# The last row of each reversed half: from the sync queue to the GpSimd queue, two steps behind the indirect store

## The chip, the cores and the metric

The kernel runs on one core of a Trainium2 chip. The metric is the device time of one execution in microseconds (us). The kernel before took 2382.77 us, the median of three runs (2381.13 to 2389.46).

## The reference

Eight batches of attention whose 12 heads are mixed before and after the softmax ("talking heads"), followed by a Fourier mixing of the result, a normalisation and a two-layer network:

```python
scores = scale * np.matmul(q, k.transpose(0, 1, 3, 2))      # q, k, v: 8 x 12 x 448 x 64
scores = np.einsum('bhij,hg->bgij', scores, w_pre)
attn = softmax(scores)
attn = np.einsum('bhij,hg->bgij', attn, w_post)
x = np.matmul(attn, v)                                      # to (8, 448, 768)
X = np.fft.fft(np.fft.fft(x, axis=1), axis=2)
u = x + np.real(X)
un = (u - mean(u)) / np.sqrt(var(u) + 1e-06)
out = u + np.maximum(un @ w_ch1, 0.0) @ w_ch2               # 768 -> 3072 -> 768
```

Everything is float32; the two weight matrices arrive as 64-bit floats and are converted on the chip.

## The kernel before, in words

There are two stages. The mixing stage computes `u` and leaves it in DRAM; the network stage (from 840 us on) reads it back and does the rest. Only the mixing stage and the passage into the network stage matter here.

**Steps.** Each batch is cut into 8 blocks of query rows and the blocks into 23 steps, so 8 batches make 184 steps. One step treats 4 x 5 rows of scores of all 12 heads. A loop over the step number `s` runs a list of actions (`ORDERS`, one list for even and one for odd `s`) and works on several steps at once:

- `emit_gather(s + 4)` (L496): four DMAs of 60 x 448 floats each (105 KB) copy the scores `Sb` of a step into the layout `Kr`, in which heads lie along partitions. All are issued by SyncE's queue (SP). `Kr` has three buffers.
- `emit_premix(s + 2)` (L507): TensorE multiplies `Kr` by the first mixing matrix, 16 small matmuls.
- `emit_max(s + 2)` (L514, VectorE), `emit_exp(s + 2)` (L521, ScalarE), `emit_scale(s + 2)` (L531, GpSimd): softmax.
- `emit_postmix(s)` (L541, TensorE) and `emit_turn(s)` (L554, VectorE): second mixing and a transposition.
- Fillers between them: the products of q and k (L479), whose results ScalarE copies to `Sb` (L342), products with v (L571), Fourier matmuls (L615, L680, L696), and the conversion of weights, one VectorE operation a step.

So a gather is issued in the loop two steps ahead of the matmuls that read it. TensorE, VectorE, ScalarE and GpSimd run exactly in the order in which the program is written; SP's queue is ordered by the framework's scheduler. GpSimd also issues the loads of q, k and v of the next batch (L425, L434), the loads and stores of weights (L225, L233) and does part of the Fourier folding (L636 to L657).

**The store.** When the last Fourier product of a batch's half has been added (`done` in `emit_s2`, L707 and L709), the closure `store` is put on the list `later`. In the `scale` action of each step, after `emit_scale`, the loop runs as many entries of `later` as stood there when the step began. `store` handles two tiles `X` of 113 rows. One goes to `u_scr` by an ordinary DMA (L728, SP). The other holds rows in reverse order and goes to `u_rev` by an indirect DMA (L719, GpSimd) that scatters 112 rows through the table `rows`. In the second half of a batch (`pair` 1) the tile has one row more, number 112, for row 112 of `u_rev`. Its DMA (L725) is what the change touches: 768 floats, once per batch, issued by SP. Because both DMAs write the tensor `u_rev[b]`, the framework lets L725 wait until the indirect store has landed.

In SP's order L725 stands behind one gather after L728 (batches 0, 2, 4) or behind two (batches 1, 3, 5), with the next gather right behind it. For batches 6 and 7 the store comes after the last step: batch 6 at the passage into the network stage, ahead of the first loads of `u` (L946, `load_u`), and batch 7 inside the first tile of the network stage. There the list `later` is emptied at once by `part`, or for batch 6 by the last turns of the loop and `part`.

Of the kernel before, what the change touches and what calls it, by code (L numbers as in the profile page):

```python
# [33 lines left out]
GR = SH // 2  # L34
# [268 lines left out]
def mix_phase(ctx, tc, rest, ident, q, k, v, w_pre, w_post, u_scr, u_rev, wts):  # L303
# [6 lines left out]
    nc = tc.nc  # L310
# [28 lines left out]
    pend, folds, later = [], [], []  # L339
# [14 lines left out]
    def ms_tile():  # L354
        return ms[-1]()
# [332 lines left out]
    def emit_s2(b, pair, par):  # L688

        st = batches[b]  # L690
        n, i0 = PR[pair], pair * GR
        ps = ms_tile()
        for y in range(2):
            w, _ = FOLD[par][par ^ y]
            for ch in range(2):
                nc.tensor.matmul(ps[:n, y:DH + 1:2],  # L696
                                 st["z", par, par ^ y][:w, ch, i0:i0 + n],
                                 tcs[:w, par, y, ch, :DQ + 1 - y],
                                 start=(ch == 0), stop=(ch == 1))

        def done():
            for back in range(2):
                X = groups[b * NG + 2 * pair + back]["X"]
                sub, add = (ALU.subtract, ALU.add) if par else (ALU.add, ALU.add)
                if back:
                    sub, add = add, sub
                nc.vector.tensor_tensor(X[:n, 0:DH + 1], X[:n, 0:DH + 1],  # L707
                                        ps[:n, 0:DH + 1], op=sub)
                nc.vector.tensor_tensor(X[:n, DH + 1:DM], X[:n, DH + 1:DM],  # L709
                                        ps[:n, DH - 1:0:-1], op=add)  # L710
            if par == 0:
                return
            later.append(store)

        def store():
            for back in range(2):
                X = groups[b * NG + 2 * pair + back].pop("X")
                if pair ^ back:
                    nc.gpsimd.indirect_dma_start(  # L719
                        out=u_rev[b][:, :],  # L720
                        out_offset=bass.IndirectOffsetOnAxis(
                            ap=rows[:GR, pair:pair + 1], axis=0),
                        in_=X[:GR, :], in_offset=None)
                    if pair:
                        later.append(lambda X=X: nc.sync.dma_start(  # L725
                            out=u_rev[b][GR:GR + 1, :], in_=X[GR:GR + 1, :]))
                else:
                    nc.sync.dma_start(  # L728
                        out=u_scr[b][pair * (SH + 1):pair * (SH + 1) + GR, :],
                        in_=X[pair:pair + GR, :])  # L730
        return [done]
# [674 lines left out]
```

## Time and profile before

| | |
|---|---|
| median of three runs | 2382.77 us |
| the profiled execution | 2392.76 us, its span 2391.0 us |
| PE / DVE / ACT / POOL busy, share of the span | 96% / 70% / 46% / 47% |
| mixing matmuls L507 | 2944, 554 ns mean, 221.2 us |
| gathers L496, all issued by SP | 736 of 105 KB; about 0.77 us of SP each |
| indirect stores L719 | 16, of 1042 ns on GpSimd; landing 4.1 to 5.9 us after their start |
| row stores L725 | 8, of 0.23 us on SP, at 255.6, 358.5, 457.3, 561.0, 663.2, 766.9, 833.6 and 915.6 us |
| loads by GpSimd in the mixing stage | L425 0.73 us, L434 0.63 us of GpSimd each |

The profiled execution took 10 us more than the median. Times inside it are counted from the span's start. PE is TensorE, DVE VectorE, ACT ScalarE, POOL GpSimd; a q behind an engine's name (SPq) means its sequencer, which issues DMAs and waits. In a timeline a bracket at the end of a row gives the idle time of the engine before it and what ended it.

### The profile page before, as it was taken

The numbers are of one execution on the slowest core, as the hardware profiler recorded it, in microseconds if no ns is written. First come the engines' busy times: TensorE is split into PE (matmuls) and PEld (weight loads), VectorE is DVE, ScalarE is ACT, GpSimd is POOL, SyncE is SP. The second block draws the span as 40 slices with busy tenths as digits, with TensorE's granted clock in tenths as the row PEclk, the third lists the DMA queues.
The fourth block names the chain that finished last, engine by engine and source line by source line (L and its number), as shares of the span: only waits on it lengthen the run. The fifth ranks groups of instructions, "written<-read, shape, count | busy, mean of one in ns | idle before, by whom it ended". The sixth has DMA issues, their size and how long they took to land.

```text
span 2391.0 us, 59448 instructions
## 1 busy us (share of the span) xinstructions
PE 2292.0 (96%) x22600; PEld 1717.7 (72%) x22600; DVE 1669.0 (70%) x3596; ACT 1100.5 (46%) x3085; POOL 1125.2 (47%) x1672
## 2 busy tenths in 40 slices
PE   6999999999999859999999999999999999999998
PEld 2455554554555547777777779999899999999998
DVE  3768786786877636776676767677767777776556
ACT  4767766676666522232122224444443444444444
POOL 3587877877776441211234343334333433344333
PEclk9999999999999979999999999999999999999999
DMA  7565554655645545656888794568466747674553
GB/s 159 158 177 175 175 176 144 198 165 163 187 156 163 203 131 169 223 189 234 242 245 218 215 307 114 165 176 242 133 161 178 219 135 189 160 219 118 146 126 67
DMA packets 213385, 425.60 MB, mean 178 GB/s; under 512 B 38766, under 2 KB 135430, under 8 KB 213102
## 3 DMA queue, kind: packets, MB, share of 16 engines
q1 hardware_dynamic: 142446, 280.38, 34.0%
q0 software_dynamic: 64656, 139.45, 26.8%
q8 instruction: 181, 2.97, 0.5%
q10 hardware_dynamic: 6000, 1.97, 0.5%
q14 instruction: 102, 0.84, 0.1%
HBM read 213.16 MB, written 129.39 MB: 143 GB/s over the span
## 4 chain that ended last, share of the span: by engine, by line
PE 52%; issue 6%; POOL 3%; DMA 2%; DVE 2%; ACT 0%; SPq 0%; POOLq 0%; DVEq 0%
PE psP L1062 15%; PE psP L1192 10%; PE psR L1062 8%; PE psR L1192 5%; PE psQ L1062 4%; PE psP L1135 4%; PE psQ L1192 3%; PE psR L1135 2%; PE psQ L1135 1%; POOL w L233 1%; DMA u<-u 1%; PE psQ L996 0%; DMA w1t<-w 0%; POOL raw L225 0%; DMA w<-wst 0%
## 5 line engine op out<-in xcount | busy, mean ns | idle before, releaser
L1062 PE MATMUL psP<-ub,w1t 128*128 128x256 f32 x2016 | 480.4, 379 | 1.2 <-DVE h L1081 1.2
L1062 PEld LDWEIGHTS psP<-ub,w1t 128*128 128x128 f32 x2016 | 379.0, 190 | 49.4 <-DVE h L1081 1.6
L531 POOL TENSOR_SCALAR PP<-PP,rcp 128x448 f32<-128x448 f32 x368 | 234.1, 645 | 230.2 <-DVE rcp L529 190.8
L514 DVE TENSOR_REDUCE nmx<-mx 128x1 f32<-128x448 f32 x368 | 213.7, 619 | 158.7 <-PE mx L507 153.7
L521 ACT ACTIVATE PP<-mx,nmx 128x448 f32<-128x448 f32 x368 | 230.3, 631 | 197.3 <-DVE nmx L514 187.4
L1226 POOL DMA_DIRECT2D out_dram<-od x109 | 132.9, 1394 | 282.5 <-DVE od L1223 159.5
L1026 POOL TENSOR_TENSOR hq<-h 128x256 f32<-128x256 f32 (+1 forms) x168 | 104.2, 620 | 292.4 <-ACT h L1082 172.0
L507 PE MATMUL mx<-Kr,kw 60*32 60x448 f32 x2944 | 221.2, 554 | 21.3 <-DMA Kr<-Sb 19.9
L1062 PE MATMUL psR<-ub,w1t 128*128 128x256 f32 x1008 | 232.9, 381 | 0.0
L1223 DVE TENSOR_TENSOR od<-od 128x768 f32<-128x768 f32 x196 | 188.6, 974 | 52.1 <-ACT od L1220 50.2
L1062 PEld LDWEIGHTS psR<-ub,w1t 128*128 128x128 f32 x1008 | 192.6, 191 | 26.4
L479 PE MATMUL ms<-kT,qT 64*32 64x448 f32 (+1 forms) x3072 | 202.3, 549 | 7.9 <-ACT qT L342 6.5
L554 DVE STREAM_TRANSPOSE Pv<-po 128x896 f32<-128x896 f32 x184 | 203.7, 1107 | 5.5 <-PE po L541 3.3
L342 ACT COPY Sb<-ms 124x448 f32<-124x448 f32 (+1 forms) x384 | 184.3, 540 | 48.8 <-PE ms L479 25.2
L541 PE MATMUL po<-PP,kw 60*32 60x448 f32 x2944 | 196.4, 541 | 0.0
L1220 ACT COPY od<-psP 128x192 f32<-128x192 f32 x390 | 124.7, 320 | 146.1 <-PE psP L1192 141.6
L571 PEld LDWEIGHTS ms<-Pv,vv 64*64 64x64 f32 x5376 | 137.0, 132 | 69.2 <-issue 52.3
L225 POOL DMA_DIRECT2D raw<-in_moe_w_ch_dram x88 | 53.4, 609 | 270.1 <-DVE tmp L269 252.4
L571 PE MATMUL ms<-Pv,vv 64*64 64x120 f32 (+1 forms) x5376 | 158.7, 263 | 0.4 <-ACT X L342 0.4
L1135 PE MATMUL psP<-w2t,h 128*128 128x384 f32 x448 | 153.8, 486 | 1.4 <-DVE od L1155 1.4
L1081 DVE TENSOR_TENSOR h<-h,psP 128x512 f32<-128x512 f32 x42 | 28.8, 687 | 142.0 <-PE psP L1062 141.6
L1135 PEld LDWEIGHTS psP<-w2t,h 128*128 128x128 f32 x448 | 84.1, 190 | 54.9 <-DVE od L1155 2.0
(143 smaller groups left out, 4497.3 us busy)
## 6 DMA issues: line engine op xcount, KB each, us to landing
ub<-ub SPq DMA_DIRECT2D x294, 384.0 KB
Kr<-Sb SPq DMA_DIRECT2D x736, 105.0 KB
out_dram<-od POOLq DMA_DIRECT2D x137, 384.0 KB, 8.7
w1t<-w SPq DMA_DIRECT2D x42, 384.0 KB
w2t<-w SPq DMA_DIRECT2D x42, 384.0 KB
raw<-in_moe_w_ch_dram POOLq DMA_DIRECT2D x56, 256.0 KB, 4.2
raw<-in_moe_w_ch_dram POOLq DMA_DIRECT2D x32, 384.0 KB, 5.0
w<-wst POOLq DMA_DIRECT2D x92, 128.0 KB, 4.3
```

Source lines behind the costliest of these rows:

```text
L479: nc.tensor.matmul(pss[x][o:o + hi - lo, :S], st["qT", xx][64 * x:64 * x + 64, y, lo:hi], st["kT", xx][64 * x:64 * x + 64, y, :], start=Tr ...
L507: nc.tensor.matmul(mx[x][64 * z + o:64 * z + o + 32, :S], kw1[64 * x:64 * x + KR, o:o + 32], Kr[64 * x:64 * x + KR, z, :], start=True, sto ...
L514: nc.vector.tensor_reduce(nmx[:, :], steps[T]["mx"][x][:, :S], axis=AX.X, op=ALU.max, negate=True)
L521: nc.scalar.activation(steps[T]["PP"][:, x, :], steps[T]["mx"][x][:, :S], ACTF.Exp, bias=steps[T]["nmx", x][:, :], accum_out=steps[T]["den ...
L531: nc.gpsimd.tensor_scalar(PP[:, x, :], PP[:, x, :], rcp[:, x:x + 1], 1.0, op0=ALU.mult, op1=ALU.mult)
L541: nc.tensor.matmul(po[o:o + 32, z, :S], kw2[64 * z:64 * z + KR, y, :], PP[64 * z:64 * z + KR, :, c * HS:(c + 1) * HS], start=True, stop=True)
L554: nc.vector.transpose(turned[a]["Pv"][:, j, :].rearrange("p (z s) -> p z s", z=2), steps[T]["po"][:, :, :S])
L571: nc.tensor.matmul(pss[y][64 * x:64 * x + 64, :nu * R], st["v", pr][64 * y:64 * y + 64, x, jb * D:(jb + 1) * D], _ap(Pv, 64 * y * rp + 32 ...
L1062: nc.tensor.matmul(p[:, m, :], w1[i][:, kc, m * P:(m + 1) * P], ub[:, kc, :], start=i in (0, 4, 1)[:3 - seed] and m == kc == 0, stop=kc == ...
L1135: nc.tensor.matmul(p, h[:, LHS[i], kf, x * P:(x + 1) * P], w2[i][:, kf, :], start=i in (0, 4, 1)[:3 - (c > 0)] and kf == 0, stop=kf == FM ...
L1192: nc.tensor.matmul(ps[j, key][:, :DQ], a, b, start=m in (0, 4), stop=True, skip_group_check=True)
L1223: eng.tensor_tensor(D[j][:, :, :], D[j][:, :, :], D[k][:, :, :], op=ALU.add)
```

## The change

The single row's DMA is issued by GpSimd instead of SP, and one level of delay is put around it: in place of the DMA itself, the list `later` gets a function that puts the DMA on `later` once more.

```diff
                     if pair:
-                        later.append(lambda X=X: nc.sync.dma_start(
-                            out=u_rev[b][GR:GR + 1, :], in_=X[GR:GR + 1, :]))
+                        later.append(lambda X=X: later.append(lambda: nc.gpsimd.dma_start(
+                            out=u_rev[b][GR:GR + 1, :], in_=X[GR:GR + 1, :])))
```

In step `t` `store` issues the indirect DMA, in `t + 1` the outer function runs, in `t + 2` the DMA is issued, after that step's two scale operations (L531). In the resulting order of instructions TensorE, VectorE and ScalarE have the same sequence as before. SP has eight DMAs fewer and gathers follow each other where L725 stood. GpSimd has eight DMAs more: in batches 0, 2 and 4 between the scale operations and the next loads of v and q, in batches 1, 3 and 5 between the scale operations and a folding operation (L636), in batch 6 behind both indirect stores, a small memset and two weight loads, with three more weight loads behind it, and in batch 7 directly behind the second indirect store. The row is written as 16 pieces of 48 floats there, where SP's form was one piece of 768. It still waits for the landing of the indirect store[...].

## Prediction

> **What bounds the kernel now.** I read the page first, then SP's waits, then the timelines of SP, TensorE and GpSimd around each row store, and last the chain of waits at the passage into the network stage. On the page TensorE is the bound nearly everywhere, and the mixing matmuls wait for gathers:
>
> ```profile
> span 2391.0 us, 59448 instructions
> ...
> L507 PE MATMUL mx<-Kr,kw 60*32 60x448 f32 x2944 | 221.2, 554 | 21.3 <-DMA Kr<-Sb 19.9
> ```
>
> With the weight loads of the same line the view by tile puts 61.6 us of TensorE's idle time down to gathers that had not landed. The next view is SP's own waits from 200 to 930 us (us in total, times, longest), the one after it the indirect store by its line:
>
> ```profile
> SPq L725 <- DMA v<-X,rows: 28.7, 8, 5.4
> ```
> ```profile
> DMA to landing us min/median/max: 4.1/4.8/5.9
> ```
>
> So SP stands still for 28.7 us in all until the indirect store has landed. Behind L725 stand gathers. SP's timeline in batch 1 (start, us, what):
>
> ```profile
> 347.37 7.05 SPq L496 DMA_DIRECT2D Kr<-Sb  x8
> 358.49 0.23 SPq L725 DMA_DIRECT2D v<-X  x1
> 358.82 21.48 SPq L496 DMA_DIRECT2D Kr<-Sb  x19
> ```
>
> Between 354.4 and 358.5 us nothing is issued. TensorE's timeline a few us later; the first row is an undisturbed step:
>
> ```profile
> 359.64 0.96 PE L507 MATMUL mx<-Kr,kw 60*32 60x448 f32 x16
> ...
> 363.67 0.94 PE L507 MATMUL mx<-Kr,kw 60*32 60x448 f32 x4
> 366.62 1.81 PE L507 MATMUL mx<-Kr,kw 60*32 60x448 f32 x8 [2.01 <-DMA Kr<-Sb]
> 368.91 0.96 PE L507 MATMUL mx<-Kr,kw 60*32 60x448 f32 x2 [0.48 <-DMA Kr<-Sb]
> ...
> 374.41 0.98 PE L507 MATMUL mx<-Kr,kw 60*32 60x448 f32 x16
> ```
>
> From one step's first L507 to the next it takes 4.03 us before (359.64 to 363.67) and 10.74 us here: 6.7 us lost. The reader should also see that the matmuls run slower afterwards. The windows view (busy of PE, PEld, DVE, ACT, POOL, then clock, DMA share, GB/s):
>
> ```profile
> 366.50:371.00 4.50, 3.90 (x32) 1.26 (x40) 0.96 (x2) 0.72 (x2) 2.03 (x3) 0.51 0.66 200
> ```
>
> The granted clock is 0.51 there; the records of the clock have 0.5 for 6.8 us from 366.6 us, and again in batch 3. Meanwhile GpSimd issues a burst of loads of the next batch[...]:
>
> ```profile
> 360.31 1.23 POOL L434 DMA_DIRECT2D vv<-in_v_dram  x2
> 361.52 1.43 POOL L425 DMA_DIRECT2D rawq<-in_q_dram  x2
> 362.99 1.40 POOL L531 TENSOR_SCALAR PP<-PP,rcp 128x448 f32<-128x448 f32 x2
> ```
>
> The last gather of the step was issued at 361.3 us and its matmuls ran at 368.9 us, a good 7 us, where the gathers of a calm stretch take two to three (by the trace's packets). At the passage into the network stage the same wait lies in the chain:
>
> ```profile
> 829.33 4.21 DMA v<-X,rows
> ...
> 833.56 0.24 SPq L725
> ...
> 833.89 9.46 DMA u<-u
> ```
>
> [...] SP issues nothing between the end of the eight gathers and the landing, 4.1 to 5.9 us after L719. [...] So a gain must come from SP's order, not from bandwidth. [...] the two stalls of 3 to 5 us (batches 1 and 3) are followed by half clock, the shorter ones are not.
>
> **The change part by part.** *Removed: eight DMAs and their wait on SP.* The issue itself is 8 x 0.23 = 1.8 us, beside other work. The wait holds SP, by batch 0 to 5, for 1.0, 4.0, 4.2, 4.3, 5.2 and 5.4 us, and for 4.6 us in batches 6 and 7 together (sum 28.7). The next gather cannot always go as early as SP is free. In batches 1, 3 and 5 it opens a new block and needs ScalarE's copies to Sb, which end at 356.25, 559.24 and 762.54 us. In batches 0, 2 and 4 it is free, but the gather after it needs a new block. The first gather behind the hold moves forward by 255.9 - 254.6 = 1.3; 358.8 - 356.3 = 2.5; 457.6 - 453.0 = 4.6; 561.4 - 559.3 = 2.1; 663.5 - 658.0 = 5.5; 767.2 - 762.6 = 4.6 us.
>
> What TensorE loses there now, from the spacing of the first L507 of neighbouring steps against the same place of a batch without a stall (4.03 to 4.1 us, for one step 3.3): batch 0 1.1 (another 1.8 there belongs to a gather that was late before L725), batch 1 6.7, batch 2 5.2, batch 3 8.6, batch 4 4.5, batch 5 1.5 us. Sum 27.6 us. About 6 of these are half clock.
>
> What stays: in batches 1 and 3 the first set now goes out before the burst (356.3 to 358.8 against loads from 359.1 on), but the second one is issued at 359.6 into it. Four gathers are 430 KB; in the burst SP's queue got some 60 KB/us by the trace's packets, so this set lands near 368.3 us, and TensorE wants it at 367.7: about 1 us is left in batch 1, and by the same sum 2 us in batch 3. [...] In batches 2 and 4 a few tenths are left.
>
> *Added: eight DMAs on GpSimd.* A plain small load from GpSimd takes 0.56 us (tables, L396), a large one 0.63 (L434): I take 0.65 each, 3.9 us in six batches. The DMA stands about 10 us behind the indirect store (batch 0: 251.2 and 261.1; batch 1: 353.7 and 364.4), and that lands within 5.9, so I expect no wait for it. [...] Queued behind it are v and q loads (needed steps later) and the next scale operation, for which TensorE's L541 waits. GpSimd is late here: the scale at 362.99 stands 3.9 us after its reciprocal. TensorE's stall hides this now. Without it L541 of that step would start at 364.4 us, when the scale ends (364.39): no slack, though the new DMA comes after it. In batch 2 the next scale moves from 466.1 to 466.8 and ends at 468.0, with L541 wanted at 467.3: 0.7 us appears. I put 1.3 us on what is late next. Bounds: 0, if loads moved later cost nothing, and 3.9 if every issue falls on TensorE. Less than nothing is excluded, as GpSimd does no less work.
>
> So the mixing stage keeps 27.6 - 1 - 2 - 0.8 - 1.3 = 22.5 us. *Batch 6*: SP issues the first loads of u at 830.4 in place of 833.9. [...] I count 2 of the 3.2 us (bounds 0 and 3.2). GpSimd waits there instead, for some 3 us; behind it are three weight loads and, at 849.7, a statistic that waits for VectorE anyway. *Batch 7*: SP's 1.4 us hold only output stores, and GpSimd's next work comes at 928.5: nothing.
>
> Sum -24 us. The profiled execution of 2392.8 would become 2369; the median 2382.8, 10 us lower, becomes 2359.
>
> **The rivals.** *Only the advance of the issue is won.* If every set still lands as long after its issue as now, the gain is the advance of the binding gather: 0.9 + 2.5 + 2.4 + 2.1 + 1.9 + 1.5 = 11.3, with 1.5 at the passage 13: 2370 us. For it: the gathers are starved by the burst, and Sb limits the odd batches. Against it: the DMA engines carry nothing of SP's from 356 to 360 us. *It was hidden anyway.* If the burst alone sets the landing, 3 us remain: 2380 us. Against it: in batches 2 and 4 the stall follows a hold of 4 to 5 us with the set issued late in full. *GpSimd becomes the bound.* If L725 waits on GpSimd in each batch, for the landing (5.9) or through slow small pieces (192 bytes each, a form that no row of before shows), it holds the next scale, whose slack is near nothing once TensorE does not stall. It decides from 4 us per batch, where the gain is eaten; slower by 12 us needs (24 + 12) / 6 = 6 us in each of six batches: 2395 us. Against it: 10 us of distance. *The change does nothing*, as the row is still issued by SP: excluded by the order of instructions.
>
> **How the numbers follow.** Forecast 0.66 (2350 to 2366), only the advance 0.17, hidden 0.10, GpSimd the bound 0.07. The range goes from 2350 (all of 27.6 + 3.2 won, less a little for the spread of runs) to 2374. About 0.5%, 12 us, is what a measurement can tell: faster means below 2371. That holds the forecast and most of the second case, 0.78; same 0.15; slower 0.07.
>
> **What would show it.** In the new trace: no SP wait on the indirect store; gathers in one chain; TensorE's wait for Kr down from 61.6 to some 30 us; no half clock near 366 and 571 us; L725 on GpSimd of about 0.65 us without a wait except in batches 6 and 7; PE waiting for PP (L531) a little more. Wrong would be: as many waits for Kr as now, or L541 waiting for GpSimd in each batch.

## The result, and the profile after

The kernel changed took 2378.98 us (median of 17 runs, 2375.72 to 2387.89), the kernel before 2387.13 us beside it (median of 17 runs, 2379.55 to 2393.89). The ratio is 0.9968, 95% interval 0.9956 to 0.9979: 7.6 us faster, with bounds of 5.0 and 10.5. The forecast had the sign right, but the gain is a third of the 24 us forecast, and 2379 lies outside the range of 2350 to 2374. It is within 0.5%, the case that had a chance of 0.15.

The page of the profile after, the two lines that were shown of before:

```profile
span 2374.9 us, 59455 instructions
...
L507 PE MATMUL mx<-Kr,kw 60*32 60x448 f32 x2944 | 213.4, 550 | 14.1 <-DMA Kr<-Sb 12.3
```

TensorE's matmuls still wait 12.3 us for gathers, where 19.9 us stood before. With the weight loads it is 39.7 us (before 61.6), by the view of the tile `Kr`:

```profile
  DMA Kr<-Sb: 39.7, 45
...
  PEld mx L507: 27.4, 34
  PE mx L507: 12.3, 11
```

What the change does to the queues is as it was read from the order. The row store by its line, now on GpSimd:

```profile
L725 POOL DMA_DIRECT2D v<-X x8: 517/554/570, 260.9 to 902.9; - x8
...
  DMA v<-X,rows: 5.5, 2
```

Eight issues of 0.55 us (min, median and max in ns), and only two of them, those of batches 6 and 7, wait for the indirect store, 5.5 us together. In SP's timeline of batch 1 no other DMA stands between the gathers any more. A row of SP's timeline runs over SP's idle times, so the second fence gives the same timeline from 354.2 us on:

```profile
347.00 0.43 SPq L728 DMA_DIRECT2D u<-X  x1
347.53 24.54 SPq L496 DMA_DIRECT2D Kr<-Sb  x25
```
```profile
356.36 4.06 SPq L496 DMA_DIRECT2D Kr<-Sb  x5
```

The hole, which lasted from 354.4 to 358.5 us, is shorter but not gone: the first gather behind the former place of L725 goes out at 356.4 us instead of 358.8, 0.1 us from where the forecast had it (356.3). Until then SP waits for ScalarE's copies (L342, 2.3 us).

TensorE's timeline for the same steps:

```profile
363.82 1.26 PE L507 MATMUL mx<-Kr,kw 60*32 60x448 f32 x14
...
367.81 0.94 PE L507 MATMUL mx<-Kr,kw 60*32 60x448 f32 x4
369.12 1.34 PE L507 MATMUL mx<-Kr,kw 60*32 60x448 f32 x10 [0.37 <-DMA Kr<-Sb]
...
373.93 0.98 PE L507 MATMUL mx<-Kr,kw 60*32 60x448 f32 x16
```

From 363.82 to 367.81 it is 3.99 us, an undisturbed step. The step that took 10.74 us before is no longer stalled; but the one after it takes 6.12 us, 2.1 too much. The windows view of these steps (PE, PEld, DVE, ACT, POOL, then clock, DMA share, GB/s) has the full clock where it was 0.51:

```profile
363.00:366.50 3.50, 3.50 (x84) 1.85 (x74) 1.99 (x6) 2.20 (x9) 3.47 (x6) 1.00 0.98 209
366.50:371.00 4.50, 4.13 (x47) 1.93 (x51) 2.76 (x7) 2.08 (x6) 4.42 (x7) 1.00 0.65 202
```

**Where the gain lies.** The first mixing matmul (L507) of the last step starts at 799.7 us, before at 812.0: 12.3 us. From there to the first matmul of the network stage (L996) it is 40.2 us, before 40.8, and from there to the end nothing that two traces of one kernel don't differ by. So all that can be seen is in the mixing stage. A second profile of each kernel (below) has 811.9 and 799.0 us for the same start: this part of the trace repeats within 1 us.

**A measure for the experiments.** For the stretch behind each row store I sum, over its five or six steps, the spacing of the first L507 from one step to the next, less the shortest spacing that eight of the traces show at the same place of a batch. It is stricter than the sum of the forecast, which came to 27.6 us for before: it counts the 1.8 us of batch 0 that the forecast set aside, and some 4 us more against the stricter comparison.

| lost behind the row store, us | b0 | b1 | b2 | b3 | b4 | b5 | sum | last step's L507 at |
|---|---|---|---|---|---|---|---|---|
| before | 2.9 | 7.9 | 5.2 | 9.9 | 4.5 | 3.0 | 33.4 | 812.0 |
| before, second profile (e4) | 2.9 | 9.2 | 4.3 | 9.2 | 3.7 | 3.3 | 32.6 | 811.9 |
| changed | 2.6 | 3.6 | 2.9 | 5.4 | 1.4 | 2.2 | 18.1 | 799.7 |
| changed, second profile (e8) | 3.4 | 2.8 | 2.9 | 4.6 | 1.3 | 2.9 | 17.9 | 799.0 |
| e2, row on ScalarE | 2.6 | 2.8 | 2.9 | 7.5 | 1.9 | 2.4 | 20.1 | 804.0 |
| e3, GpSimd, no delay | 8.6 | 7.2 | 6.1 | 5.6 | 4.6 | 3.6 | 35.7 | 816.6 |
| e5, no row | 2.3 | 3.8 | 3.0 | 5.1 | 2.3 | 1.6 | 18.1 | 800.8 |
| e6, changed, q and v loads later | 1.0 | 1.3 | 4.0 | 2.8 | 0.0 | 1.6 | 10.7 | 791.3 |
| e7, before, q and v loads later | 1.2 | 4.4 | 3.3 | 7.0 | 2.8 | 4.3 | 23.0 | 804.7 |
| e9, changed, q load later | 2.5 | 2.4 | 2.5 | 4.0 | 0.7 | 1.9 | 14.0 | 790.2 |
| e10, changed, v load later | 2.6 | 2.8 | 4.2 | 3.6 | 1.0 | 1.9 | 16.1 | 797.6 |
| e11, GpSimd, one step | 2.6 | 5.8 | 3.4 | 7.3 | 2.4 | 1.8 | 23.3 | 803.2 |

The change takes the loss from 33 to 18 us. The forecast left 3.8 us, which is 9.6 in this measure (3.8 + 1.8 + 4.0), if those 5.8 us stay as they were. So the question for the experiments is what the other 8.4 us are.

TensorE's wait for `Kr` can be split in the same way. In the six steps behind each store it was 35.9 us before and is 13.0 after the change (30.9 and 14.4 in the second profiles). The rest of the 61.6 and 39.7 us, about 26 us in each of the four profiles, lies elsewhere in the stage, where the change does nothing.

**The stretch that kept most, batch 3.** TensorE's timeline after the change:

```profile
562.30 0.97 PE L507 MATMUL mx<-Kr,kw 60*32 60x448 f32 x12
565.01 0.74 PE L507 MATMUL mx<-Kr,kw 60*32 60x448 f32 x2 [1.74 <-DMA Kr<-Sb]
...
569.99 1.12 PE L507 MATMUL mx<-Kr,kw 60*32 60x448 f32 x16
```

From 562.30 to 569.99 it is 7.69 us, 3.7 more than a step. The chain of waits there (start, us, what):

```profile
556.46 0.77 SPq L496
...
557.27 7.69 DMA Kr<-Sb
564.96 0.04 issue
565.01 0.74 PE mx L507 x2
```

A DMA's piece of the chain begins when its issue begins. So TensorE waited for the last gather of the first set behind the former place of L725. SP issued the set from 554.8 us on, this gather at 557.27, and it landed 7.69 us later. GpSimd's timeline shows what was under way:

```profile
555.62 0.65 POOL L434 DMA_DIRECT2D vv<-in_v_dram  x1
556.32 1.26 POOL L531 TENSOR_SCALAR PP<-PP,rcp 128x448 f32<-128x448 f32 x2
557.53 0.62 POOL L233 DMA_DIRECT2D w<-wst  x1
558.15 0.55 POOL L225 DMA_DIRECT2D raw<-in_moe_w_ch_dram  x1
558.70 1.22 POOL L434 DMA_DIRECT2D vv<-in_v_dram  x2
559.91 1.44 POOL L425 DMA_DIRECT2D rawq<-in_q_dram  x2
```

And the windows view of the same microseconds has the 16 DMA engines busy nearly all the time (last two columns share and GB/s):

```profile
557.00:560.00 3.00, 3.00 (x80) 1.50 (x80) 2.01 (x6) 2.03 (x9) 3.00 (x6) 1.00 0.85 220
560.00:562.00 2.00, 2.00 (x68) 1.34 (x56) 1.97 (x5) 2.00 (x6) 1.97 (x3) 1.00 0.85 240
562.00:565.00 3.00, 1.26 (x28) 0.30 (x18) 0.87 (x2) 1.46 (x7) 2.97 (x6) 1.00 1.04 223
```

Being issued ahead of most of the burst did not help: seven GpSimd loads and stores went out between 1.7 us ahead of this gather's issue and 4.1 us behind it, six of them behind, and the share of the 16 engines was 0.85 to 1.04 while it was on its way.

Which set is hit is not fixed. In the second profile of the changed kernel (e8) the same traffic stands at the same place, but the first set comes in time for the start of its step. The wait is on the next set, which SP issues into the burst:

```profile
559.66 9.40 DMA Kr<-Sb
```

That step takes 7.46 us (566.15 to 573.61).

### The profile page after: what moved, and what is told of

Read it like the earlier page. It is cut to its first block, busy times and chain, and to the rows that moved or that the text cites. A ratio compares the mean times of both kernels' runs of the same rounds, so it can differ in the third digit from the quotient of the medians.

```text
span 2374.9 us, 59455 instructions
## 1 busy us (share of the span) xinstructions
PE 2282.5 (96%) x22600; PEld 1716.0 (72%) x22600; DVE 1677.3 (71%) x3596; ACT 1102.4 (46%) x3085; POOL 1130.8 (48%) x1680
## 4 chain that ended last, share of the span: by engine, by line
PE 76%; issue 7%; DMA 5%; POOL 4%; DVE 4%; ACT 3%; SPq 1%; ACTq 0%; POOLq 0%; DVEq 0%
PE psP L1062 15%; PE psP L1192 10%; PE psR L1062 8%; PE mx L507 6%; PE psR L1192 5%; PE ms L571 5%; PE ms L479 5%; PE psQ L1062 4%; PE po L541 4%; PE psP L1135 4%; DMA Kr<-Sb 3%; PE psQ L1192 2%; PE psR L1135 2%; PE ms L696 2%; ACT PP L521 1%
## 5 line engine op out<-in xcount | busy, mean ns | idle before, releaser
L531 POOL TENSOR_SCALAR PP<-PP,rcp 128x448 f32<-128x448 f32 x368 | 234.5, 647 | 214.7 <-DVE rcp L529 172.7
L507 PE MATMUL mx<-Kr,kw 60*32 60x448 f32 x2944 | 213.4, 550 | 14.1 <-DMA Kr<-Sb 12.3
L1062 PEld LDWEIGHTS psR<-ub,w1t 128*128 128x128 f32 x1008 | 192.6, 191 | 26.4
L479 PE MATMUL ms<-kT,qT 64*32 64x448 f32 (+1 forms) x3072 | 202.4, 547 | 9.3 <-ACT qT L342 6.6
L342 ACT COPY Sb<-ms 124x448 f32<-124x448 f32 (+1 forms) x384 | 184.4, 540 | 39.5 <-PE ms L479 24.5
L541 PE MATMUL po<-PP,kw 60*32 60x448 f32 x2944 | 197.1, 541 | 0.3 <-DVE rcp L528 0.2
```

The lines of the kernel that those rows point to most:

```text
L479: nc.tensor.matmul(pss[x][o:o + hi - lo, :S], st["qT", xx][64 * x:64 * x + 64, y, lo:hi], st["kT", xx][64 * x:64 * x + 64, y, :], start=Tr ...
L507: nc.tensor.matmul(mx[x][64 * z + o:64 * z + o + 32, :S], kw1[64 * x:64 * x + KR, o:o + 32], Kr[64 * x:64 * x + KR, z, :], start=True, sto ...
L531: nc.gpsimd.tensor_scalar(PP[:, x, :], PP[:, x, :], rcp[:, x:x + 1], 1.0, op0=ALU.mult, op1=ALU.mult)
L541: nc.tensor.matmul(po[o:o + 32, z, :S], kw2[64 * z:64 * z + KR, y, :], PP[64 * z:64 * z + KR, :, c * HS:(c + 1) * HS], start=True, stop=True)
L1062: nc.tensor.matmul(p[:, m, :], w1[i][:, kc, m * P:(m + 1) * P], ub[:, kc, :], start=i in (0, 4, 1)[:3 - seed] and m == kc == 0, stop=kc == ...
```

## The experiments

Three theories stood for what ate the rest. **B, the burst:** the q and v loads that GpSimd issues in the same 5 us keep the gathers late, whatever SP does. (By the packets of the changed kernel's trace GpSimd's queue moved 177 KB/us and SP's 53 from 560 to 565 us, 27 and 168 from 366 to 371 us.) **G, GpSimd:** the eight new DMAs delay GpSimd and through L541 TensorE. **H, the profile:** the execution that the forecast was read from lost more than an ordinary one, so there was less to win. Each ratio is to the kernel before, run on the same chip beside it.

**e1: the row inside the indirect store.** Meant as a ceiling: no DMA of its own, on no queue.

```diff
-                            ap=rows[:GR, pair:pair + 1], axis=0),
-                        in_=X[:GR, :], in_offset=None)
+                            ap=rows[:PR[pair], pair:pair + 1], axis=0),
+                        in_=X[:PR[pair], :], in_offset=None)
                     if pair:
-                        later.append(lambda X=X: nc.sync.dma_start(
-                            out=u_rev[b][GR:GR + 1, :], in_=X[GR:GR + 1, :]))
+                        pass
```

> The row has no DMA of its own: in the second half of a batch the indirect store scatters 113 rows in place of 112, so neither SP nor GpSimd issues L725 and nobody waits for the landing. Theory G (the eight DMAs on GpSimd eat most of the gain): clearly faster than the changed kernel, ratio to the kernel before about 0.992 (-19 us). Theory B (the gathers that run into the burst of loads of q and v set what is left, whoever stores the row): same as the changed kernel, ratio 0.996 to 0.998, and TensorE still waits some 40 us for Kr. Theory H (only the one profiled execution had such long stalls, the typical one has about half): also 0.996 to 0.998, and a repeated profile of the kernel before shows less than 61.6 us of waits for Kr.

Measured: 2455.86 us, ratio 1.0285 (1.0260 to 1.0309). None of the ranges expected holds, and it is no ceiling, since the indirect store itself changed. Its landing by its line, then TensorE's wait behind it, in the tile `vv` (a part of the answer) and in the timeline:

```profile
DMA to landing us min/median/max: 3.8/21.8/22.6
```
```profile
  DMA vv<-in_v_dram: 71.0, 8
```
```profile
275.40 3.82 PE L571 MATMUL ms<-Pv,vv 64*64 64x120 f32 x56 [9.11 <-DMA vv<-in_v_dram]
```

With 113 rows the store lands after some 22 us, with 112 rows in the kernel before after 4.1 to 5.9. The v loads queued behind it on GpSimd land after 13.7 us in the median (4.4 before), and TensorE waits 71 us for them. Why one row more makes it some 22 us in place of 4.8 in the median is not shown. e1 says nothing about the theories.

**e2: the row on ScalarE's queue, two steps behind.** Takes the eight DMAs off GpSimd and off SP.

```diff
-                        later.append(lambda X=X: nc.sync.dma_start(
-                            out=u_rev[b][GR:GR + 1, :], in_=X[GR:GR + 1, :]))
+                        later.append(lambda X=X: later.append(lambda: nc.scalar.dma_start(
+                            out=u_rev[b][GR:GR + 1, :], in_=X[GR:GR + 1, :])))
```

> The row goes through ScalarE's queue, two steps behind the store, so GpSimd has no more work than before the change and SP has no hold. G: faster than the changed kernel by 5 us or more (ratio 0.994 or less). B and H: ratio 0.996 to 0.998 as the changed kernel, with a few tenths of a us per batch on ScalarE.

Measured: 2381.28 us, ratio 0.9974 (0.9960 to 0.9987), no different from the changed kernel. Of its later end of the mixing stage (804.0 us) some 5 us arise ahead of the first row store; behind the stores it loses 2 us more than the changed kernel, all of it in batch 3. Without GpSimd's DMAs nothing is won: against G.

**e3: GpSimd, directly behind the indirect store.** The queue changes, the delay does not come with it.

```diff
-                        later.append(lambda X=X: nc.sync.dma_start(
-                            out=u_rev[b][GR:GR + 1, :], in_=X[GR:GR + 1, :]))
+                        nc.gpsimd.dma_start(
+                            out=u_rev[b][GR:GR + 1, :], in_=X[GR:GR + 1, :])
```

> The row goes through GpSimd's queue directly behind the indirect store, without the two steps: GpSimd now waits for the landing, about 4 to 5 us in each of eight batches, ahead of its scale operations. If a hold of GpSimd costs TensorE as the forecast's rival said (slack near nothing), 3 to 5 us per batch come back: slower than the kernel before by 5 to 15 us (ratio 1.002 to 1.006). If GpSimd has slack there: ratio 0.996 to 1.000.

Measured: 2391.4 us, ratio 1.0009 (0.9994 to 1.0023): as slow as before, between the two ranges that were expected. GpSimd now stands where SP stood. Its waits at L725, its timeline in batch 1, and TensorE's timeline:

```profile
  DMA v<-X,rows: 32.1, 8
```
```profile
362.38 1.04 POOL L719 DMA_INDIRECT v<-X,rows  x1 [0.18 <-issue]
...
368.22 0.55 POOL L725 DMA_DIRECT2D v<-X  x1 [4.79 <-DMA v<-X,rows]
```
```profile
368.35 0.96 PE L507 MATMUL mx<-Kr,kw 60*32 60x448 f32 x16
...
373.17 1.75 PE L541 MATMUL po<-PP,kw 60*32 60x448 f32 x16 [3.86 <-POOL PP L531]
```

The gathers come in time (TensorE's wait for `Kr` falls to 28.2 us, with none of it in the six steps behind each store), and the scale operation behind L725 is late instead: L541 waits 50.6 us for it, against 7.7 before. The hold has moved to another engine, at nearly the same price. So the new queue alone gives nothing; with the distance to the indirect store it gives the gain.

**e4: the kernel before once more.** For H.

> The kernel before once more, for a second profile. H: TensorE waits clearly less than 61.6 us for Kr (40 to 55) and the steps behind the row stores in batches 1 and 3 lose less than 6.7 and 8.6 us. Against H: the same waits within 3 us, and then the sum of 27.6 us was typical and the change itself leaves more than was counted.

Measured: ratio 1.0 (0.9979 to 1.0021). TensorE's timeline in batch 3 of this second profile, and SP's wait:

```profile
568.28 0.94 PE L507 MATMUL mx<-Kr,kw 60*32 60x448 f32 x4
574.13 1.82 PE L507 MATMUL mx<-Kr,kw 60*32 60x448 f32 x10 [4.91 <-DMA Kr<-Sb]
```
```profile
SPq L725 <- DMA v<-X,rows: 28.5, 8, 5.4
```

The same stalls at the same places: 32.6 us lost against 33.4, 28.5 us of SP's wait against 28.7. The wait for `Kr` is 57.7 us, 3.9 less than in the first profile. That is a little more than the 3 us allowed for, but not the 40 to 55 us that H expected. The loss that the forecast was read from repeats from one profiled execution to the next: H falls for profiles. Ordinary runs leave no such view.

**e5: no row at all.** Row 112 of each batch's reversed half isn't stored from `X`. In its place one row of q is written there once, at the start.

```diff
+        for b in range(B):
+            nc.gpsimd.dma_start(out=u_rev[b][GR:GR + 1, :],
+                                in_=_ap(q, 0, [[DM, 1], [1, DM]]))
...
-                    if pair:
-                        later.append(lambda X=X: nc.sync.dma_start(
-                            out=u_rev[b][GR:GR + 1, :], in_=X[GR:GR + 1, :]))
```

> The row is left out: row 112 of each batch's reversed half is not stored from X (one row of q is put there once at the start, so that something is read), nobody issues L725 and nobody waits for the landing. It is the most that the change could win. If the new DMAs on GpSimd cost little: ratio 0.995 to 0.998 as the changed kernel, with 38 to 45 us of waits for Kr left. If they cost much: 0.993 or less. If the forecast's sum were right: 0.990.

Measured: 2378.71 us, ratio 0.9966 (0.9949 to 0.9983). From the view of the tile `Kr`:

```profile
  DMA Kr<-Sb: 50.0, 58
```

This is the ceiling that e1 failed to be. Without the row the kernel loses the same 18.1 us behind the former places of the store, and takes the same time as the changed one within the interval. The change won all that the row could give, as far as these runs can tell, and what remains does not need the row: G is out. The wait for `Kr` is above the 38 to 45 us that were expected. Of it 17.1 us lie in the six steps behind each place of the store (13.0 in the changed kernel) and 32.9 elsewhere; why there are more elsewhere was not traced, and the stage ends only 1 us later.

**e6, e7, e9, e10: the loads of q and v spread.** Tables say at which steps of a batch the loads are issued; the fourth q load and the third v load were moved. The whole edit of e6, beside the change:

```diff
-AT_L = ((-4, -3), (-2, -1), (0, 1), (2, 7), (11, 12), (13, 14))
-AT_V = ((3, 4), (5, 6), (7, 7))
+AT_L = ((-4, -3), (-2, -1), (0, 1), (2, 9), (11, 12), (13, 14))
+AT_V = ((3, 4), (5, 6), (7, 8))
```

e7 has these two lines with the kernel before, e9 only the first line with the change, e10 only the second with the change.

> The changed kernel with two of the loads of each batch moved: the second half of the last v tile one step later (7 to 8) and the second half of a q tile two steps later (7 to 9), so that four loads no longer start in one step behind the row store. If the burst is what keeps the late gathers late (theory B): TensorE's waits for Kr fall from 39.7 to below 28 us and the loss in the steps behind the stores of batches 0 to 5 from about 17 to below 9; ratio to the kernel before 0.990 to 0.994. If not: same as the changed kernel, 0.996 to 0.998.

> The kernel before with the same two loads moved, the row still on SP with its hold of about 28 us in all. If a hold costs time only together with the burst (B): most of the 31 us of loss behind the stores goes, ratio 0.993 to 0.996, at or below the changed kernel. If the hold alone delays the gathers beyond their slack: small gain, 0.997 to 1.000.

> The changed kernel with the q load alone moved (7 to 9), the v loads as before. If it is the number of loads in the one step that starves the gathers, two of four loads less bring most of the gain of both moves: ratio to the kernel before 0.991 to 0.994, and no wait of TensorE for v tiles. If the v tile is what mattered: 0.995 to 0.997.

> The changed kernel with the v load alone moved (7 to 8). One of four loads (the largest, 229 KB) leaves the step, and TensorE waits about 0.8 us for it in some batches, as with both moved: ratio 0.994 to 0.997, between the changed kernel and the one with both loads moved.

| | us | ratio to before | wait for `Kr`, us |
|---|---|---|---|
| e6, both moves, with the change | 2369.78 | 0.9923 (0.9904 to 0.9943) | 33.1 |
| e9, q load alone, with the change | 2370.12 | 0.9935 (0.9916 to 0.9955) | 30.2 |
| e10, v load alone, with the change | 2378.40 | 0.9958 (0.9943 to 0.9973) | 38.4 |
| e7, both moves, without the change | 2381.34 | 0.9968 (0.9955 to 0.9982) | 47.4 |

The ratios of e6, e9 and e10 lie in the ranges expected. The wait and the loss of e6 (33.1 and 10.7 us) fell less than expected (below 28 and 9). e7 lies between its two ranges: neither does the hold cost time only together with the burst, nor is it all that costs.

In the six steps behind each store the wait for `Kr` goes from 13.0 us (14.4 in e8) to 4.3 (e6), 7.9 (e9) and 7.8 (e10), and the loss from 18 to 10.7, 14.0 and 16.1. That is what B says. SP issues the same DMAs in the same order in all of these. GpSimd's order changes beyond the loads, since a step with a q load runs one folding operation and not two, and some of these now run a step earlier. But TensorE's wait for GpSimd's scale is not what shrinks (L541 for L531: 8.6 us in the changed kernel, 8.6 in e6, 11.4 in e9).

No single load explains it. Batch 3 of e9, first GpSimd's timeline, then the chain of waits:

```profile
552.16 1.24 POOL L434 DMA_DIRECT2D vv<-in_v_dram  x2
...
554.61 0.57 POOL L725 DMA_DIRECT2D v<-X  x1
...
560.77 1.49 POOL L425 DMA_DIRECT2D rawq<-in_q_dram  x2
```
```profile
550.74 7.83 DMA Kr<-Sb
558.58 0.04 issue
558.62 0.57 PE mx L507 x2
```

The q load is issued 6.2 us behind L725 instead of 2.8 us ahead of it, and this gather of the first set is as late as before: 7.83 us to land, against 7.69 in the first profile of the changed kernel, beside the v and weight loads alone. The step still takes 6.20 us instead of 7.69, and no half clock follows this stall. The windows view behind the two stalls, the changed kernel first, then e9, has the clock as the third figure from the end:

```profile
565.00:570.00 5.00, 4.99 (x45) 2.31 (x45) 2.40 (x5) 1.53 (x4) 2.90 (x4) 0.66 0.66 179
```
```profile
558.60:561.90 3.30, 3.28 (x43) 1.61 (x43) 2.11 (x5) 1.51 (x4) 3.22 (x6) 1.00 0.65 208
```

A single stretch tells little here: the first set of batch 3 costs 0.3 us in e6, but nothing in e8 either. It is the sums over six batches that fall in e6, e9 and e10.

By the times the move of the q load carries the gain; the v load's move alone can't be told from the changed kernel. By the traces it is less clear: of the 9.5 us by which e9 ends the mixing stage earlier than the changed kernel, 4.1 lie behind the row stores, and where the others come from was not traced. e6 and e9 can't be told apart; they are faster than the changed kernel and than the kernel before, and the best versions that ran.

e7 shows that the two causes are nearly independent. SP's hold costs 33.4 - 18.1 = 15.3 us of loss with the loads where they are, and 23.0 - 10.7 = 12.3 with them spread.

**e8: the changed kernel once more.**

> The changed kernel once more for a second profile. The loss behind the stores of batches 0 to 5 should again be 15 to 19 us (16.6 in the first), the last mixing matmul at 799 to 804 us.

Measured: 2378.11 us, ratio 0.9960 (0.9947 to 0.9973), a gain of 9.6 us that agrees with the first comparison. In its profile 17.9 us are lost. (The expectations of e6 to e8 speak of 16.6 or 17 us for the changed kernel and of 31 for the kernel before, by an earlier comparison.)

**e11: GpSimd, one step behind.** The delay is halved.

```diff
-                        later.append(lambda X=X: nc.sync.dma_start(
+                        later.append(lambda X=X: nc.gpsimd.dma_start(
```

> The row on GpSimd one step behind the indirect store in place of two. By the changed kernel's trace it then comes to stand about 5 us behind the start of the store, where the landing takes 4 to 6: GpSimd waits 0 to 1.5 us per batch (with none of the two steps it waited 32.1 us in all). Ratio 0.996 to 0.998 if the second step is worth little, 0.998 to 1.000 if even such a short hold of GpSimd reaches TensorE.

Measured: 2379.57 us, ratio 0.9968 (0.9951 to 0.9984). L725 waits for the indirect store in four of eight cases:

```profile
  DMA v<-X,rows: 10.1, 4
```

and TensorE's L541 waits 9.6 us for the scale, by its line. The trace loses 5 us more than the changed kernel's behind the row stores, but the time is the same within the interval. The second step of delay is worth nothing that these runs can measure.

Not tried: the row kept on SP but later. In the order of instructions the scheduler puts it at the same place even when the list holds it back. So what the distance alone would give on SP is not shown.

## Why the prediction failed in size and held in kind

**Right: what is removed.** SP's wait on the indirect store, 28.7 us, is gone. The first set behind it goes out as soon as `Sb` is there, the stall of batch 1 (10.74 us for a step) is an undisturbed step of 3.99, and the granted clock near 366 us is 1.00 in the changed kernel's first profile. The wait for `Kr` went from 61.6 us to 39.7 where some 30 were forecast; the difference lies behind the row stores, where 13.0 us remain.

**Right: the loss itself.** What stood at 27.6 us in the forecast, 33.4 by the measure above, comes again in e4 (32.6).

**Wrong: "What stays".** This is the term of the sum that failed. It put 1 us on batch 1, 2 us on batch 3 and a few tenths on batches 2 and 4, 3.8 us in all. By the measure above 9.6 were forecast and 18.1 and 17.9 measured, so the term is short by 8.4 us. By batch, the forecast is here the loss before, less what the forecast took from it, with its 0.8 us for batches 2 and 4 split evenly:

| us | b0 | b1 | b2 | b3 | b4 | b5 |
|---|---|---|---|---|---|---|
| forecast | 1.8 | 2.2 | 0.4 | 3.3 | 0.4 | 1.5 |
| changed | 2.6 | 3.6 | 2.9 | 5.4 | 1.4 | 2.2 |
| changed, second profile (e8) | 3.4 | 2.8 | 2.9 | 4.6 | 1.3 | 2.9 |

The reasons that it gave were of the right kind and too narrow. First, it let only sets issued *into* the burst suffer ("the first set now goes out before the burst"). In batch 3 of the first profile the first set still landed 7.69 us after its issue; in the second profile it was the set that the forecast named, with a gather that landed after 9.40 us. Secondly, it priced a late set by its lateness at the first matmul. In batch 1 the forecast had the second set land near 368.3 us and be wanted at 367.7. It was wanted at 367.81; its third gather landed at 369.08, and the step lost 2.1 us, as its weight loads waited twice for gathers, 1.17 and 0.52 us, and the work behind them moved along. Thirdly, batch 2 was put at next to nothing and missed by the most, 2.5 us: there a gather issued at 460.89 us landed 7.42 us later.

Fourthly, the forecast expected no half clock near 571 us. In the first profile 3.4 us at half clock (from 565.3 us on) follow the stall of batch 3, in which TensorE's matmuls stood still for 1.74 us. Stalls of 2.01 us (e8) and 1.95 us (e9) in the same batch are followed by none (in e9 the granted clock is 1.00 from 558.60 to 561.90 us; in e8 11 matmuls of L479 take 0.76 us at 571.25, ten at clock 1.00 in batch 1 of the first profile 0.75), so in these profiles the length of the stall alone does not tell. The stalls of batches 1 and 3 before, which the forecast called 3 to 5 us long, were 2.01 and 3.73 us of the matmuls, 2.81 and 4.54 of the weight loads; in batch 4 the weight loads stood still for 2.68 us, and no half clock followed.

e5 shows that this remainder does not need the row; e6 and e9 show that it shrinks when the burst is thinned. The 10.7 us left in e6 were not traced.

The forecast also had "a gain must come from SP's order, not from bandwidth", an estimate that no run had shown. For the change it held. But e6 and e9 left SP's order alone and took some 8 to 9 us more, by spreading the same transfers over time.

**Wrong: 2 us at the passage (batch 6).** SP's first load of `u` does go out sooner, 18.8 us behind the first mixing matmul of the last step in place of 21.9. The first statistic of the network stage starts 26.4 us behind that matmul (before 31.7), but the fourth 35.7 (before 36.3). In between the chain of waits has two landings, with SP waiting on the first to issue more. The second took 3.48 us before:

```profile
820.33 8.07 DMA u<-v
...
828.99 6.32 DMA u<-u
```

The first matmul (L996) comes 40.2 and 40.5 us behind in the two profiles after, 40.8 and 39.3 in the two before: nothing gained. The forecast's lower bound of 0 was the value.

**About right: 1.3 us on GpSimd.** Each issue took 0.55 us, not 0.65. TensorE's L541 waits 8.6 and 9.8 us for L531 in the two profiles (7.7 in both before). e2 and e5, without these DMAs, are no faster: what they cost is below what the runs can tell. The forecast's statement that GpSimd would not wait except in batches 6 and 7 held exactly. **Right: batch 7, nothing.**

**The sum.** The forecast's terms come to 24.5 us, which it rounds to 24. Less 8.4 (what stays) and 2 (passage) it is 14.1 us, all of it in the mixing stage, where the two pairs of profiles show 12.3 and 13.0; the rest is not accounted for. The ordinary runs differ by 7.6 and 9.6 us in the two comparisons. The profiled executions of the kernel before took 2392.76 and 2387.90 us, above the medians of their runs (2387.13 and 2387.73), those of the changed kernel 2376.62 and 2376.90, below theirs (2378.98 and 2378.11). The 17 runs of the kernel before spread over 14 us, so two executions of each can well differ by some 5 us more than the medians do (an estimate from that spread). That the profile itself plays a part is not shown.

**The rivals.** "It was hidden anyway" had the time nearest to the result (2380), but not the mechanism: it left 3 us of the loss to win, and the traces show 15. That its time comes near is luck: it counts from 2382.77 us, the median of three runs, and the 17 runs beside the changed kernel gave 2387.13. "Only the advance of the issue" (13 us) comes out nearest to the profiles; its reading, that a set still lands late after an early issue, is what batch 3 of the first profile shows, though not the first set of batch 1. "GpSimd becomes the bound" needed a wait on GpSimd in each batch; e3 makes that wait, and even then the time only returns to that of before, since the late gathers go at the same time.

## What to carry to other kernels

When a queue is freed from a wait, ask what other transfers will be under way beside those behind it before putting the whole stall down as won: in batch 3 of the changed kernel a gather whose issue began 1.4 us ahead of two v and two q loads (557.27 against 558.70 us) took 7.69 us to land. Look for the two causes apart: take the waiting transfer out altogether (the ceiling), and move the other traffic alone. A DMA that waited for another's landing held the queue that it stood in, SP's for 28.7 us and GpSimd's for 32.1. How far it stood behind the start of that other counted for more than the queue in these runs: on GpSimd the ratio was 1.0009 directly behind it and 0.9968 two steps behind, on ScalarE 0.9974 two steps behind.

## What the runs showed of the hardware

- The indirect store of 113 rows of 768 floats (e1) took some 22 us to land and up to 2.49 us of GpSimd to issue; that of 112 rows 4.1 to 5.9 us (before) or 3.7 to 7.3 us (changed kernel) and 1.04 us.
- A 105 KB gather took 2.6 us in the median from its issue to its last packet in a calm stretch (380 to 440 us, before); single ones took 7.69 and 7.81 us in the changed kernel and 9.40 in e8 beside GpSimd's loads, with 202 to 240 GB/s in all in the changed kernel's stretches.
- The 3 KB row as 16 pieces through GpSimd took 0.55 us to issue and 2.9 to 7.1 us to land (changed kernel).
- A DMA that waited for a landing held the queue that it stood in: SP's for 28.7 us in eight waits (before), GpSimd's for 32.1 us in eight (e3).
- Half clock (3.4 us) followed a stall of TensorE's matmuls of 1.74 us in the first profile of the changed kernel, and none followed 2.01 us (e8) and 1.95 us (e9) in the same batch.
